# Loading k and q of batches 3 to 7 in slot order, without the ScalarE permutes, and a gate ahead of each k load

## Chip, cores, metric

One core of one Trainium2 chip. The metric is the device time of one execution in microseconds (us), the median over several runs. The engines are PE (TensorE), ACT (ScalarE), DVE (VectorE), POOL (GpSimd) and SP (SyncE); in the views PEld is PE's loading of weights, and SPq is SP's issuing of a DMA. All times of whole kernels here are of fast runs; there were no slow ones (the kernel `isolated` ran once and has no state).

## The reference

```python
# q, k, v: (8 batches, 8 heads, 576 rows, 64), float32
kv  = np.einsum('bhsd,bhse->bhde', k, v)
out = np.einsum('bhsd,bhde->bhse', q, kv)
out = out / np.sqrt(np.mean(out * out, axis=-1, keepdims=True) + 1e-06) * g_norm
x = out.transpose(0, 2, 1, 3).reshape(8, 576, 512)
xn = (x - mu) / np.sqrt(var + 1e-06) * g_ln                       # mean and variance of each row of x
result = x + np.maximum(xn @ w_ch1, 0.0) @ w_ch2                  # 512 -> 2048 -> 512
```

The two large products of the last line are most of PE's work. The attention ahead of them is small, but each 128-row tile needs its q transposed, which is where the changed loads come in.

## The kernel before

A batch's 512 rows lie on 128 partitions, four rows ("slots" t = 0 to 3) to a partition; the last 64 rows come in a load of their own. k and q are loaded by head (1024 rows of 256 elements, cast from float32 to bf16 on the way), and ACT then permutes them from (head, slot) to (slot, head) order, so that one slot of two heads is one 128x128 matmul operand:

```python
def load_kv(buf, src, b, h0=0, h1=H):      # 128 partitions x 8 heads = 1024 rows of 4 x 64 elements
    ...
        nc.gpsimd.dma_start(
            kv_view(buf, b)[:, h0:h1, :, :].rearrange("p h t d -> p h (t d)"),
            src[b, h0:h1, 0:n, :].rearrange("h (p t) d -> p h (t d)", t=t))

def k_permute(eng, b, h0, h1):             # half of the heads: 128x1024 on ACT; q_permute is alike
    ...
    copy(eng, kp[b % 2][0:src.shape[0], 0:t, h0:h1, :],
         src[:, h0:h1, :, :].rearrange("p h t d -> p t h d"))

def q_turn_dma(b):                         # "the turn": a DMA transpose, issued by SP
    att[b]["qT"] = work.tile([128, 20, 128], bf16, tag="qT", name="qT", bufs=3)
    nc.sync.dma_start_transpose(
        att[b]["qT"], qp[b % 2].rearrange("p t h d -> p (t h d)"))
```

The order of the instructions on each engine isn't the order of the source. Every operation is a step with estimated durations, and a small list scheduler lays the steps out in time before the program is emitted:

```python
def run_plan():
    ...
    def ready(s):
        r = 0.0
        ...
        for d in s.deps:
            if d.done is None:
                return None
            r = max(r, d.done + (s.lag if d.dma else 0.0))   # lag: extra time granted to a load
        ...
    ...                                     # for each engine: the earliest ready step, ties by key
```

So the place of a permute among ACT's other instructions follows from when the plan expects its load to have landed. The chip then runs that order whatever the load really does. Batch b's part of the plan, cut:

```python
            gate(f - 7 if b > 3 else 5)      # POOL copies one element of a tile's xT: a wait
            gate_turn()                      # b == 3 only: POOL waits for the turn of batch 2
            pool_load(("k", b), load_kv(kb, k, b), rate4, dk)
            ...
            def some_q():
                gate(f - 6 if b > 3 else 6)
                pool_load(("q", b), load_q(b, 0, 4), rate4, [adone[b - 1]["qread"]])
                ...
            def some_v():
                gate(f - 5 if b > 3 else 7)
                pool_load(("v", b), load_kv(vb, v, b), rate4, dk)
                ...
            for h0, h1 in ((0, 4), (4, 8)):
                kperm.append(add("ACT", 0.85, 1.0, ok - 16, load["k", b][0:1] + dk,
                                 lambda h0=h0, h1=h1: k_permute(nc.scalar, b, h0, h1)))
            ...                              # two q permutes in the same way
            for x in kperm + qperm:
                x.lag = 4.0 if b == 2 else 6.0
            ...
            turn = add_dma("SP", ok - 12, qperm + load["q", b] + (...),
                           lambda: q_turn_dma(b), 2.6e3, 1.0, occ=2.98, lat=0.25, tail=0.42)
```

A second DMA transpose, "the x turn" (xT<-xc), turns the normalized rows for the first-layer matmuls. It stands in SP's order too.

Of the kernel before, what the change touches and what calls it, by code (L numbers as in the profile page):

```python
# [14 lines left out]
def kernel(  # L15
# [11 lines left out]
    nc = tc.nc  # L27
# [6 lines left out]
    B, H, S, D = q.shape  # L34
# [27 lines left out]
    def no_fifth(b):  # L62
        return fifth(b + 1)
# [30 lines left out]
    def add(eng, occ, dur, key, deps, fn, dma=None, alloc=None, main=False, lag=0.0):  # L94
        s = Step()
        s.eng, s.occ, s.dur, s.key, s.fn = eng, occ, dur, key, fn
        s.deps = [d for d in deps if d is not None]
        s.dma, s.alloc, s.main, s.frees, s.behind = dma, alloc, main, None, None
        s.start = s.done = None
        s.lag = lag  # L100
        steps.append(s)
        return s
# [76 lines left out]
    def act_cost(n):  # L179
        return n / 1400 + 0.115, n / 1400 + 0.23  # L180
# [4 lines left out]
    def add_dma(eng, key, deps, fn, nbytes, rate, occ=None, lat=None, tail=None):  # L185
        if eng == "POOL":
            s = add(eng, occ or 0.67, 0, key, deps, fn, dma=(1.0, nbytes / rate / 1e3, 0.6))
        else:
            s = add(eng, occ or 0.55, 0, key, deps, fn,
                    dma=(0.6 if lat is None else lat, nbytes / rate / 1e3,  # L190
                         0.75 if tail is None else tail))
        return s
# [21 lines left out]
    kb = [consts.tile([128, H * 6 * D], bf16, name=f"kb{i}") for i in range(2)]  # L214
# [3 lines left out]
    kp = [consts.tile([128, 6, H, D], bf16, name=f"kp{i}") for i in range(2)]  # L218
    qp = [consts.tile([128, 5, H, D], bf16, name=f"qp{i}") for i in range(2)]
    mark = consts.tile([128, 1], bf16, name="mark")  # L220
    kv_pack = [consts.tile([128, HP, 128], bf16, name=f"kv_pack{i}") for i in range(3)]

    def kv_view(buf, b):
        if b < 2:
            return buf[b % 2][0:96, :].rearrange("p (h t d) -> p h t d", h=H, t=6)
        return buf[b % 2][:, 0:H * 4 * D].rearrange("p (h t d) -> p h t d", h=H, t=4)

    def load_kv(buf, src, b, h0=0, h1=H):
        t = 6 if b < 2 else 4
        n = 576 if b < 2 else 512  # L230
        def fn():
# [3 lines that stand above are left out]
        return fn, n * (h1 - h0) * 256  # L235

    def load_q(b, t0, t1):
        def fn():
            nc.gpsimd.dma_start(
                qb[:, :, t0:t1, :].rearrange("p h t d -> p h (t d)"),  # L240
                q[b, :, 0:512, :].rearrange("h (p t) d -> p h t d", t=4)[:, :, t0:t1, :]
                .rearrange("p h t d -> p h (t d)"))
        return fn, 128 * H * (t1 - t0) * 256
# [7 lines left out]
    def load_slot(dst, src, b, t, h0=0, h1=H):  # L251
        def fn():
            nc.gpsimd.dma_start(
                dst[:, t, h0:h1, :],
                src[b, h0:h1, 0:512, :].rearrange("h (p t) d -> p t h d", t=4)[:, t, :, :])
        return fn, 128 * (h1 - h0) * 256


    groups = []
# [24 lines left out]
    att = [dict() for _ in range(B)]  # L284
    done = [dict() for _ in range(N_TILES)]
    adone = [dict() for _ in range(B)]


    rate6, rate4, rate1 = 400.0, 395.0, 305.0
# [24 lines left out]
    def pool_load(name, fnb, rate=425.0, deps=()):  # L314
        fn, nb = fnb
        s = add_dma("POOL", 0, deps, fn, nb, rate)
        load.setdefault(name, []).append(s)
# [59 lines left out]
    def k_permute(eng, b, h0, h1):  # L377
        src = kv_view(kb, b)
        t = src.shape[2]
        copy(eng, kp[b % 2][0:src.shape[0], 0:t, h0:h1, :],  # L380
             src[:, h0:h1, :, :].rearrange("p h t d -> p t h d"))
# [275 lines left out]
    def plan_batch(b):  # L657
        p = pos[FIRST[b]]
        ok = okey[FIRST[b]]
        kperm = []  # L660
        if b == 1:
            for h0, h1 in ((0, 4), (4, 8)):
                kperm.append(add("ACT", 1.2, 1.35, p - 18, load["k", 1],
                                 lambda h0=h0, h1=h1: k_permute(nc.scalar, 1, h0, h1)))
            for t in range(5):
                key = (p - 17 + 3 * t) if t < 4 else pos[8] - 40
                if t < 4:
                    qperm = add("ACT", *act_cost(512), key, load["q", 1],
                                lambda t=t: q_permute(nc.scalar, 1, t, t + 1))
                    qread = qperm  # L670
                else:
                    qperm = load["q", 1, 4][0]
                add_q_turn_pe(1, t, [qperm, z1[1]], key + 1, ("DVE", "ACT")[t % 2])
            vdeps = load["v", 1]
            adone[1]["qread"] = qread
            adone[1]["qfree"] = adone[1]["qT", 4][0]
        else:
            f = FIRST[b]
            def gate(n):

                if b >= 3:
                    m, i = divmod(n, 4)
                    pool_do(0.1, lambda: nc.gpsimd.tensor_copy(  # L683
                        mark, blk[m]["xT"][:, 0, i * 128:i * 128 + 1]), done[n]["xT"])
            def gate_turn():
                if b == 3:
                    pool_do(0.1, lambda: nc.gpsimd.tensor_copy(
                        mark, att[2]["qT"][:, 0, 0:1]), [adone[2]["qfree"]])
            dk = [adone[b - 2]["kvmm"]]
            if b < 4:  # L690

                pool_do(0.5, lambda: nc.gpsimd.memset(kp[b % 2][no_fifth(b), 4, :, :], 0.0), dk)
            gate(f - 7 if b > 3 else 5)
            gate_turn()
            pool_load(("k", b), load_kv(kb, k, b), rate4, dk)
            pool_load(("k", b), load_fifth(kp[b % 2][:, 4, :, :], k, b), 180.0, dk)
            def some_q():
                gate(f - 6 if b > 3 else 6)
                pool_load(("q", b), load_q(b, 0, 4), rate4, [adone[b - 1]["qread"]])
                pool_load(("q", b), load_fifth(qp[b % 2][:, 4, :, :], q, b), 180.0,  # L700
                          [adone[b - 2]["qfree"]])
            def some_v():
                gate(f - 5 if b > 3 else 7)
                pool_load(("v", b), load_kv(vb, v, b), rate4, dk)
                pool_load(("v", b), load_fifth(v5[b % 2], v, b), 100.0, dk)
            for load_some in (some_v, some_q) if b == 2 else (some_q, some_v):
                load_some()
            for h0, h1 in ((0, 4), (4, 8)):
                kperm.append(add("ACT", 0.85, 1.0, ok - 16, load["k", b][0:1] + dk,
                                 lambda h0=h0, h1=h1: k_permute(nc.scalar, b, h0, h1)))  # L710
            qperm = []
            for t0, t1 in ((0, 2), (2, 4)):
                qperm.append(add("ACT", 0.85, 1.0, ok - 14, load["q", b][0:1] + [
                    adone[b - 2]["qfree"]], lambda t0=t0, t1=t1: q_permute(nc.scalar, b, t0, t1)))
            for x in kperm + qperm:
                x.lag = 4.0 if b == 2 else 6.0
            kperm += load["k", b]
            turn = add_dma("SP", ok - 12, qperm + load["q", b] + (
                adone[b - 3].get("outs", []) if b >= 3 else []),
                           lambda: q_turn_dma(b), 2.6e3, 1.0, occ=2.98, lat=0.25, tail=0.42)  # L720
            for t in range(5):
                adone[b]["qT", t] = [turn]
            adone[b]["qfree"] = turn
            adone[b]["qread"] = qperm[-1]
            vdeps = load["v", b]
        outs_before = adone[b - 3].get("outs", []) if b >= 3 else []
        s = add("PE", 1.12 if b > 1 else 1.34, 1.35 if b > 1 else 1.57, (p - 17.5 if b == 1 else ok - 4), vdeps + kperm,
                lambda: kv_mm(b, range(HP)), alloc="kvt")
        a = add("DVE", 0.34, 0.38, (p - 17 if b == 1 else ok - 2), [s, z1[4], z1[5]] + outs_before,
                lambda: kv_out(b, 0, HP, nc.vector, False))  # L730
        a2 = add("DVE", 0.34, 0.38, (p - 17 if b == 1 else ok - 2), [a], lambda: kv_out(b, 0, HP, nc.vector, True))
        s.frees = a2
        s.lag = 5.0 if b > 2 else 2.0 if b == 2 else 0.0
        adone[b]["kvmm"] = s
        adone[b]["kv"] = [a2]
# [203 lines left out]
```

## Time and profile before

| | before |
|---|---|
| time, median of 3 runs | 298.25 us (298.1 to 299.0) |
| span of the profiled run | 297.3 us |
| PE busy / ACT busy / POOL busy | 282.9 / 159.3 / 54.9 us |
| PE waits listed after 53 us | 1.8 us (ACT) and 0.9 us (turn of batch 3) |

PE's idle time and its waits, with their lines, are read in the prediction. Two cautions for that reading. The profiled run took 299.07 us, more than any of the three timed ones, so its waits may be on the long side. And this trace holds 2017 of PE's 2045 matmul records, and a missing record looks like idle time. I therefore also use a measure that needs no matmul record, the time from the first attention product after 53 us to the start of the last DVE eviction (an eviction takes a matmul's result out of PSUM). Before, it is 239.48 us (53.74 to 293.22). I call it **the stretch**.

### The profile page before, as it was taken

How to read it: one execution, taken by the hardware profiler on the slowest of the kernel's cores; microseconds unless marked ns; L12 is line 12 of the kernel's file. 1: busy time of each engine (PE TensorE's matmuls, PEld its weight loads, DVE VectorE, ACT ScalarE, POOL GpSimd, SP SyncE). 2: the span in 40 equal slices, each digit the busy share in tenths (PEclk: the TensorE clock that was granted, in tenths of full speed). 3: DMA queues.
4: the chain of work that ended last, by engine and by line, in shares of the span. 5: the costliest groups of instructions: out<-in, count | busy, mean ns of one | idle time of the engine just before them, and what ended most of it. 6: DMA issues, size and time to landing. Idle time of an engine off the chain costs nothing.

```text
span 297.3 us, 5131 instructions
## 1 busy us (share of the span) xinstructions
PE 282.9 (95%) x2017; PEld 162.3 (55%) x2045; DVE 165.9 (56%) x359; ACT 159.3 (54%) x308; POOL 54.9 (18%) x88
## 2 busy tenths in 40 slices
PE   3999999999998999799999999999999999999994
PEld 1889955977754445344454444544454444444443
DVE  1497048669695778176754875577557755420022
ACT  3178963978977942594169517841762177016400
POOL 8873320206020122310212020220000000000000
PEclk9999999999999999999999999999999999999999
DMA  7999999549979999994788959888201310120012
GB/s 97 181 200 205 204 198 196 153 90 134 174 134 127 115 113 191 163 155 93 143 129 99 168 143 132 99 92 218 55 18 53 90 53 19 55 90 16 0 73 71
DMA packets 75932, 35.21 MB, mean 118 GB/s; under 512 B 44547, under 2 KB 71427, under 8 KB 75908
## 3 DMA queue, kind: packets, MB, share of 16 engines
q0 software_dynamic: 41888, 18.35, 51.5%
q1 hardware_dynamic: 33860, 16.39, 23.6%
q8 instruction: 16, 0.26, 0.4%
q10 hardware_dynamic: 160, 0.13, 0.2%
q14 instruction: 8, 0.07, 0.1%
HBM read 36.70 MB, written 9.44 MB: 155 GB/s over the span
## 4 chain that ended last, share of the span: by engine, by line
PE 82%; DMA 10%; ACT 2%; issue 1%; DVE 1%; POOL 1%; POOLq 0%
PE mm_ps L609 36%; PE mm_ps L590 28%; PE mm_ps L575 9%; DMA kb<-in_k_dram 3%; PE out_ps L444 3%; DMA qT<-qp 3%; PE kv_ps L421 2%; DMA qp<-in_q_dram 2%; DMA xT<-xc 2%; PE idle_ps L892 1%; ACT m L597 1%; PE qT_ps L393 1%; PE xT_ps L525 1%; POOL kb L232 0%; ACT sq L457 0%
## 5 line engine op out<-in xcount | busy, mean ns | idle before, releaser
L609 PE MATMUL mm_ps<-w,m 128*128 128x512 bf16 (+1 forms) x577 | 129.3, 373 | 0.7
L590 PE MATMUL mm_ps<-xT,w 128*128 128x512 bf16 x435 | 99.8, 379 | 2.4 <-ACT m L597 1.8
L609 PEld LDWEIGHTS <-m 128*128 128x128 bf16 x592 | 56.7, 98 | 59.8
L597 ACT ACTIVATE m<-mm_ps 128x512 bf16<-128x512 f32 x112 | 65.6, 597 | 43.0 <-PE mm_ps L590 42.1
L590 PEld LDWEIGHTS <-w 128*128 128x128 bf16 x448 | 43.1, 98 | 50.6 <-issue 2.1
L466 DVE TENSOR_REDUCE ss<-sq 128x8 f32<-128x512 f32 (+1 forms) x37 | 24.8, 669 | 49.8 <-ACT sq L457 49.8
L616 DVE SCALAR_TENSOR_TENSOR x<-mm_ps,rstd,x 128x512 f32<-128x512 f32 (+1 forms) x37 | 27.1, 734 | 40.0 <-PE mm_ps L609 39.9
L457 ACT ACTIVATE sq<-out_ps 128x512 f32<-128x512 f32 (+1 forms) x37 | 21.5, 585 | 49.4 <-PE out_ps L444 49.4
L575 PE MATMUL mm_ps<-xT,w 128*128 128x128 bf16 x512 | 30.9, 219 | 0.7 <-ACT xT L532 0.7
L575 PEld LDWEIGHTS <-w 128*128 128x128 bf16 x512 | 29.3, 98 | 1.5 <-issue 0.8
L518 DVE SCALAR_TENSOR_TENSOR xc<-x,mv,gl 128x512 bf16<-128x512 f32 (+1 forms) x37 | 27.1, 737 | 1.2
L461 DVE TENSOR_TENSOR xg<-out_ps,gn 128x512 f32<-128x512 f32 (+1 forms) x37 | 24.7, 669 | 0.3
L683 POOL COPY mark<-xT 128x1 bf16<-128x1 bf16 x15 | 5.0, 331 | 100.7 <-DMA xT<-xc 85.3
L582 ACT ACTIVATE m<-mm_ps 128x512 bf16<-128x512 f32 x32 | 18.3, 597 | 2.6 <-PE mm_ps L575 1.9
L496 DVE TENSOR_TENSOR x<-xg,inv 128x512 f32<-128x512 f32 x24 | 16.6, 692 | 0.8
L373 ACT COPY kp<-kb 128x1024 bf16<-128x1024 bf16 (+1 forms) x14 | 15.2, 1102 | 3.2 <-DMA kb<-in_k_dram 3.2
L512 DVE BATCH_NORM_STATS2 stats<-x 128x6 f32<-128x512 f32 x24 | 16.6, 690 | 0.5
L444 PE MATMUL out_ps<-kv_pack,qT 128*128 128x128 bf16 x160 | 15.1, 221 | 1.1 <-DMA qT<-qp 0.9
L444 PEld LDWEIGHTS <-qT 128*128 128x128 bf16 x160 | 11.6, 99 | 8.1 <-DMA qT<-qp 1.4
L470 ACT ACTIVATE rms<-ss,eps_attn 128x8 f32<-128x8 f32 (+1 forms) x37 | 11.1, 300 | 8.7 <-DVE ss L466 8.7
L436 DVE CAST kv_pack<-kv_ps 64x256 bf16<-64x256 f32 (+1 forms) x18 | 7.1, 392 | 13.4 <-PE kv_ps L421 13.1
L421 PE MATMUL kv_ps<-vb,kp 128*128 128x128 bf16 (+1 forms) x144 | 11.7, 234 | 2.6 <-DMA vb<-in_v_dram 2.6
(59 smaller groups left out, 172.6 us busy)
## 6 DMA issues: line engine op xcount, KB each, us to landing
out_dram<-x SPq DMA_DIRECT2D x32, 256.0 KB, 3.0
w<-in_moe_w_ch_dram POOLq DMA_DIRECT2D x8, 512.0 KB, 12.2
qb<-in_q_dram POOLq DMA_DIRECT2D x7, 512.0 KB, 7.4
kb<-in_k_dram POOLq DMA_DIRECT2D x6, 512.0 KB, 8.8
vb<-in_v_dram POOLq DMA_DIRECT2D x6, 512.0 KB, 7.2
out_dram<-x SPq DMA_DIRECT2D x6, 128.0 KB, 2.4
qp<-in_q_dram POOLq DMA_DIRECT2D x10, 64.0 KB, 6.7
kb<-in_k_dram POOLq DMA_DIRECT2D x2, 288.0 KB, 5.8
```

The costliest lines, as they stand in the source:

```text
L421: nc.tensor.matmul(ps[:, hp, :], lhsT=kp[b % 2][p, t, 2 * hp:2 * hp + 2, :].rearrange("p h d -> p (h d)"), rhs=(v5[b % 2][:, 2 * hp:2 * hp ...
L444: nc.tensor.matmul(o3[:, hp, :], lhsT=att[b]["qT"][:, 4 * t + hp, :], rhs=kv_pack[b % 3][:, hp, :], start=(i == 0), stop=(i == len(bs) - 1))
L457: nc.scalar.activation(sq[:, h0:h1, :], st[n]["ps", h0][:, h0:h1, :], func=AF.Square)
L461: nc.vector.tensor_mul(xg[:, h0:h1, :], st[n]["ps", h0][:, h0:h1, :], gn.to_broadcast([128, h1 - h0, D]))
L466: nc.vector.tensor_reduce(ss[:, h0:h1, :], st[n]["sq"][:, h0:h1, :], axis=AX.X, op=ALU.add)
L518: nc.vector.scalar_tensor_tensor(xc[:, f0:f1], in0=st[n]["x"][:, f0:f1], scalar=blk[m]["mv"][:, i, 0:1], in1=gl[:, f0:f1], op0=ALU.subtrac ...
L575: nc.tensor.matmul(ps[:, d, :], lhsT=w1[c][:, kk, d * 128:(d + 1) * 128], rhs=blk[m]["xT"][:, kk, i * 128:(i + 1) * 128], start=(kk == 0), ...
L582: nc.scalar.activation(st[n]["m1"][:, c, :, :], st[n]["m1ps", c], func=AF.Relu)
L590: nc.tensor.matmul(ps, lhsT=w1[c][:, kk, d * 128:(d + 1) * 128], rhs=blk[m]["xT"][:, kk, :], start=(kk == 0), stop=(kk == nKm - 1))
L597: nc.scalar.activation(blk[m]["m1", c][:, d, :], blk[m]["m1ps", g], func=AF.Relu)
L609: nc.tensor.matmul(st[n]["m2ps", f0], lhsT=m1_piece(n, c, d), rhs=w2[c][:, d, f0:f1], start=(c == 0 and d == 0), stop=(c == 3 and d == 3))
L616: nc.vector.scalar_tensor_tensor(x[:, f0:f1], in0=st[n]["m2ps", f0], scalar=blk[m]["rstd"][:, i, :], in1=x[:, f0:f1], op0=ALU.mult, op1=AL ...
```

## The change

Its intent: take 20 permutes off ACT by letting the DMA write k and q in slot order, and keep each k load from running beside the turn of the batch in front. Its diff, with the repeated parts cut:

```diff
+    def load_slots(dst, src, b):
+        def fn():
+            nc.gpsimd.dma_start(
+                dst[:, 0:4, :, :],
+                src[b, :, 0:512, :].rearrange("h (p t) d -> p t h d", t=4))
+        return fn, 128 * H * 4 * 256
...
             def gate_turn():
-                if b == 3:
+                if b >= 3:
                     pool_do(0.1, lambda: nc.gpsimd.tensor_copy(
-                        mark, att[2]["qT"][:, 0, 0:1]), [adone[2]["qfree"]])
+                        mark, att[b - 1]["qT"][:, 0, 0:1]), [adone[b - 1]["qfree"]])
...
-            pool_load(("k", b), load_kv(kb, k, b), rate4, dk)
+            by_slot = b >= 3
+            if by_slot:
+                pool_load(("k", b), load_slots(kp[b % 2], k, b), rate1, dk)
+            else:
+                pool_load(("k", b), load_kv(kb, k, b), rate4, dk)
...
-                pool_load(("q", b), load_q(b, 0, 4), rate4, [adone[b - 1]["qread"]])
+                if by_slot:
+                    pool_load(("q", b), load_slots(qp[b % 2], q, b), rate1, [adone[b - 2]["qfree"]])
+                else:
+                    pool_load(("q", b), load_q(b, 0, 4), rate4, [adone[b - 1]["qread"]])
...
-            for h0, h1 in ((0, 4), (4, 8)):
+            for h0, h1 in ((0, 4), (4, 8))[by_slot * 2:]:
...
-            for t0, t1 in ((0, 2), (2, 4)):
+            for t0, t1 in ((0, 2), (2, 4))[by_slot * 2:]:
...
+            turn.lag = 5.0 if by_slot else 0.0
-            adone[b]["qread"] = qperm[-1]
+            adone[b]["qread"] = qperm[-1] if qperm else None
```

`[by_slot * 2:]` leaves an empty tuple, so that no permute is made. With `turn.lag` the plan lets the turn follow its loads with 5 us to spare; until now it was the permutes that it granted this (`x.lag`).

The diff moves line numbers by 7: L373 becomes L380, L413 L420 (the turn), L421 L428 (k-v product), L444 L451 (attention product), L536 L543 (x turn), L590 L597 (first-layer matmul), and so on. L597 is thus the Relu eviction on ACT in the kernel before, and the first-layer matmul in the kernel after.

## The prediction

> **What bounds the kernel now.** I read the page's busy table first, then PE's waits by stage, then the timeline around each wait.
>
> ```profile
> PE 282.9 (95%) x2017; PEld 162.3 (55%) x2045; DVE 165.9 (56%) x359; ACT 159.3 (54%) x308; POOL 54.9 (18%) x88
> ```
>
> PE is busy for 95% of the span; ACT, whose work the change removes, for 54%. Less ACT work alone is therefore worth nothing; only what ACT makes PE wait for counts. The page warns that a busy PE need not be at its peak. Here it is close: in the timeline, groups of four 128x512 matmuls follow each other every 0.864 us, 216 ns for 512 columns, and the granted clock was 1.00 in all slices. The next view is the table by stage. It covers batches 3 to 7, and then the tail.
>
> ```profile
> core 0: us, PE busy (x) PEld busy (x) DVE busy (x) ACT busy (x) POOL busy (x), PEclk, DMA share, GB/s
> 53.00:297.00 244.00, 236.19 (x1488) 125.09 (x1509) 137.43 (x277) 128.15 (x243) 29.08 (x48) 1.00 0.63 104
> 255.00:297.00 42.00, 37.97 (x189) 18.67 (x191) 6.22 (x9) 9.55 (x16) 0.00 (x0) 0.99 0.16 54
> ```
>
> From 53 us on PE is idle for 244.00 - 236.19 = 7.81 us. Of these 42.00 - 37.97 = 4.03 us lie in the last window, nearly all of it the last eviction and store after the last matmul, which the change doesn't touch. What is left is 7.81 - 4.03 = **3.8 us: the most that any change of these loads can win**. PE's list of waits says where:
>
> ```profile
> PE mm_ps L590 <- ACT m L597: 1.8, 1, 1.8
> ...
> PE out_ps L444 <- DMA qT<-qp: 0.9, 1, 0.9
> ```
>
> One wait of 1.8 us for the Relu eviction, one of 0.9 us for the turned q of batch 3. The other three waits of that list end before 53 us. The first in the timeline:
>
> ```profile
> 123.21 1.04 ACT L373 COPY kp<-kb 128x1024 bf16<-128x1024 bf16 x1 [3.23 <-DMA kb<-in_k_dram]
> 124.16 1.56 ACT L597 ACTIVATE m<-mm_ps 128x512 bf16<-128x512 f32 x3
> 124.81 5.56 PE L590 MATMUL mm_ps<-xT,w 128*128 128x512 bf16 x24 [1.78 <-ACT m L597]
> ```
>
> A k permute of batch 5 stands in ACT's order ahead of evictions that are ready. Its k load was issued at 112.94 and landed 10.25 us later, so ACT stood still for 3.23 us, no PSUM bank of the first layer came free, and PE ran dry for 1.78 us. The load itself was in no hurry: batch 5's k is first multiplied at 148.8. The second:
>
> ```profile
> 81.41 1.98 ACT L373 COPY qp<-qb 128x1024 bf16<-128x1024 bf16 x2
> ...
> 83.64 3.20 SPq L413 DMA_TRANSPOSE qT<-qp  x1
> ...
> 85.39 0.88 POOL L232 DMA_DIRECT2D kb<-in_k_dram  x1
> ...
> 91.68 0.40 PE L444 MATMUL out_ps<-kv_pack,qT 128*128 128x128 bf16 x4 [0.90 <-DMA qT<-qp]
> ```
>
> The turn of batch 3 was issued at 83.64, after the permutes and an output store, and landed 8.00 us later, the slowest of the six (minimum 5.0, median 6.5). The k load of batch 4 was issued 1.75 us after it and ran on the same engines.
>
> **What the Trainium skill says.** (1) "PSUM — Partial Sum Buffer", section "Engine vs sequencer instructions": "ScalarE/VectorE/GpSimdE queues are strict FIFO." The trace agrees: the 3.23 us stand of ACT with evictions behind it. (2) "ScalarE: Activation LUTs", "What ACT_TABLE_LOAD costs": 186 ns plus 0.833 ns an element, so 1039 ns for 1024 elements; the trace has 1042 ns for the permutes. (3) "DMA: Bandwidth & Descriptors", "Specifications" and "Bandwidth": line rate wants transfers of at least 512 B, and the floor of a small load is put at about 10.5 ns a packet. I take that as the price of one more short packet on an engine; no row of this trace isolates it. (4) The same page, "Issuing engines are not separate DMA queues": loads and turns share the 16 engines. The 8.00 us turn beside a load fits.
>
> **The change part by part.**
> Removed on ACT: 4 permutes for each of 5 batches, 20 x 1.042 = **20.8 us of ACT**, of which only the 1.78 us wait (batch 5) and the hold on the batch 3 turn touch PE. ACT should go from 159.3 to about 138.5.
> Added in the loads: ten of them are now cut by head and slot, 128 x 32 = 4096 rows of 64 elements instead of 128 x 8 = 1024 rows of 256. Software-queue packets should grow by 10 x 3072 = 30,720, from 41,888 to 72,608, with the same bytes. An engine gets 256 packets instead of 64, each 256 B read and 128 B written. By the skill's 10.5 ns the 192 further packets are about 2.0 us a load (estimate, upper side, as part of a packet's time is spent on bytes anyway).
> Added on POOL: issuing 512 rows took 688 ns and 1024 rows 882 ns, 0.38 ns a row. By that slope 4096 rows need 882 + 3072 x 0.379 = 2.05 us (estimate), 1.17 us more for each of ten, and four further marks of 0.2 to 0.7 us: POOL goes from 54.9 to about 68, far from a bound.
> Moved: k loads of batches 4 to 7 wait for the turn in front. Only batch 4's is really held, from 85.4 to about 89; batch 5's from 112.9 to about 115. Their k is needed at 117 and 149. On PE the order changes in one place: the k-v product of batch 3 comes two groups (1.73 us) later, still two groups ahead of its first use, so its 0.85 us of kv_pack casts should just fit. On SP the turn of batch 5 moves ahead of one x turn.
>
> Is a q load now late for its turn? Issue of q to issue of the turn was 15.3, 12.3, 14.5, 11.1 and 9.6 us for batches 3 to 7. The new load needs 7.4 (median landing before) + 1.2 (issue) + 2.0 (packets) = 10.6 us. Only batch 7 misses, by 1.0 us, and before 195.85 its turn waited for the permutes anyway. The x turn behind it went out at 201.51; landings in that stage took at most 4.9 us, so it was there by 206.4, and the next block starts at 207.58: 1.2 us to spare. That just holds it.
>
> Sum: 1.78 + 0.90 = 2.7 us won on PE, nothing lost. 298.25 - 2.7 = **295.6 us**, 0.9% faster.
>
> **The rivals.**
> A: *the short rows become the new wait.* If slot loads land in 15 us instead of 10.6, the turn of batch 7 comes 5.4 us late, the x turn behind it in SP's order too, and PE waits some 4 us; batch 6, with 4.5 us to spare at its block, loses little. That gives 295.6 + 4 = about 300. For it: the page's DMA share already stands at 8 or 9 tenths in several slices. Against: bytes are the same, the k loads have 30 us of room, and no k load now competes with the turn in front.
> B: *ACT was a brake everywhere*, so that all 20.8 us matter and the time falls by more than 2%. Against: 3.8 us is all the idle time that PE has outside start and tail; to win 6 us is impossible unless the matmuls themselves become faster.
> C: *the wait moves.* The 1.78 us stall goes, but batch 3's first product then waits for the later k-v product or the casts behind other DVE work (about 0.5 us), or the 0.9 us wait remains since the output store still stands ahead of the turn on SP. That gives 296.5 to 297.5.
>
> **Range and chances.** The ceiling gives 298.25 - 3.8 = 294.5 as the best; timing noise before was 298.1 to 299.0. C sets most of the upper side, A the tail. Range 294.2 to 297.8. Within 2% means 292.3 to 304.2: faster needs the impossible B, 0.02; slower needs an A larger than I can build, 0.03; same 0.95.
>
> **What would show it.** Right: no permutes of 128x1024 after 53 us except batch 2's four, ACT near 138.5; no wait of PE on L597's counterpart near 124 and none at batch 3's first product; about 72,600 packets on the software queue; slot loads of about 2 us issue on POOL and about 10 us to landing; the k load of batch 4 after the turn landed, and that turn nearer 6 us than 8. PE's busy time unchanged at 283, its idle time from 53 us to the tail about 1 us. Wrong: a new PE wait for an x turn or qT (rival A), one for kv_pack (C), or shorter matmuls (B).

## The result, and the profile after

| | before | after |
|---|---|---|
| time, median, same chip | 298.18 us (297.62 to 299.0, 4 runs) | 295.95 us (295.5 to 296.31, 4 runs) |
| ratio of fast runs | | 0.9922 (95%: 0.9894 to 0.9951) |
| profiled span | 297.3 us | 294.5 us |
| the stretch | 239.48 us | 237.39 us |
| ACT / POOL busy | 159.3 / 54.9 us | 143.1 / 66.1 us |

A ratio is the mean time of one kernel's fast runs over that of the other's in the same rounds, so not quite the ratio of the medians. The change is 0.8% faster, which counts as the same at 2%. Of the 2.8 us between the two spans, 2.09 us lie in the stretch. Most of the rest (0.68 us) comes before 53 us, where the change touches nothing: the first attention product after 53 us starts at 53.06 instead of 53.74. I don't count that.

The busy line of the page after:

```profile
PE 283.4 (96%) x2045; PEld 161.2 (55%) x2045; DVE 165.7 (56%) x359; ACT 143.1 (49%) x288; POOL 66.1 (22%) x92
```

PE's work is the same, and ACT has 20 instructions fewer. The software queue, before and after (packets, MB, share of the engines' span):

```profile
q0 software_dynamic: 41888, 18.35, 51.5%
```

```profile
q0 software_dynamic: 72608, 18.35, 64.8%
```

30,720 more packets for the same bytes, the number worked out in advance. PE's waits after (line, what for, us in total, times, longest):

```profile
PE kv_ps L428 <- DMA vb<-in_v_dram: 3.0, 1, 3.0
PE scale_ps L307 <- DMA scales<-in_moe_g_ln_dram: 2.2, 1, 2.2
PE mm_ps L597 <- DMA xT<-xc: 0.8, 1, 0.8
```

These are the three longest. The first two lie in the start-up and stood there before. The waits of 1.8 and 0.9 us are both gone; the third line is new. First the one that went, in the timeline around the turn of batch 3 after (start, us, instruction, and in brackets the idle time before it with its releaser):

```profile
82.33 3.23 SPq L420 DMA_TRANSPOSE qT<-qp  x1
...
88.08 0.19 POOL L694 COPY mark<-qT 128x1 bf16<-128x1 bf16 x1 [4.18 <-DMA qT<-qp]
88.76 2.02 POOL L260 DMA_DIRECT2D kp<-in_k_dram  x1 [0.49 <-PE kv_ps L428]
...
89.95 0.39 PE L451 MATMUL out_ps<-kv_pack,qT 128*128 128x128 bf16 x4
```

The turn is issued 1.31 us earlier than before (83.64), as no permute stands ahead of it (0.68 us of this is the earlier start of everything), and lands after 5.6 us instead of 8.0. The mark on POOL is the added gate: it waits 4.18 us for the turn, so the k load of batch 4 goes out at 88.76 instead of 85.39. PE's first product of the batch at 89.95 has no wait.

Then the new wait, in batch 6. Before:

```profile
162.58 0.88 POOL L232 DMA_DIRECT2D vb<-in_v_dram  x1 [0.27 <-issue]
...
166.18 3.62 SPq L413 DMA_TRANSPOSE qT<-qp  x1
169.89 1.22 SPq L536 DMA_TRANSPOSE xT<-xc  x1
```

After:

```profile
163.52 0.89 POOL L232 DMA_DIRECT2D vb<-in_v_dram  x1 [0.42 <-issue]
163.65 3.38 SPq L420 DMA_TRANSPOSE qT<-qp  x1
167.12 2.19 SPq L543 DMA_TRANSPOSE xT<-xc  x1
...
174.80 4.48 PE L597 MATMUL mm_ps<-xT,w 128*128 128x512 bf16 x20 [0.76 <-DMA xT<-xc]
```

On the clock the turn goes out 2.5 us earlier, and the v load 0.9 us later. But PE is 3.7 us ahead by now (its attention product of 167.61 stands at 163.93): measured by PE's work the turn goes out 1.2 us later, and the v load 4.6 us. They used to be 3.6 us apart; now they start together. The turn lands after 10.4 us (5.1 before), and the x turn behind it after 7.43 us (2.5 before), 0.76 us too late for PE. The chain of work that ended last runs through it:

```profile
167.12 7.43 DMA xT<-xc
174.55 0.25 issue
174.80 4.48 PE mm_ps L597 x20
```

### The profile page after: what moved, and what is told of

It reads as the page before. It is cut to its first block, busy times and chain, and to the rows that moved or that the text cites. A ratio compares the mean times of both kernels' runs of the same rounds, so it can differ in the third digit from the quotient of the medians.

```text
span 294.5 us, 5143 instructions
## 1 busy us (share of the span) xinstructions
PE 283.4 (96%) x2045; PEld 161.2 (55%) x2045; DVE 165.7 (56%) x359; ACT 143.1 (49%) x288; POOL 66.1 (22%) x92
## 3 DMA queue, kind: packets, MB, share of 16 engines
q0 software_dynamic: 72608, 18.35, 64.8%
## 4 chain that ended last, share of the span: by engine, by line
PE 87%; DMA 7%; POOL 3%; DVE 1%; issue 1%; ACT 0%; ACTq 0%; POOLq 0%
PE mm_ps L616 39%; PE mm_ps L597 33%; PE mm_ps L582 8%; DMA w<-in_moe_w_ch_dram 5%; PE kv_ps L428 3%; PE out_ps L451 3%; DMA xT<-xc 3%; POOL qp L253 1%; POOL w L333 1%; PE xT_ps L532 1%; POOL kb L232 1%; POOL vb L232 0%; PE qT_ps L400 0%; DVE ss L473 0%; DVE x L503 0%
## 5 line engine op out<-in xcount | busy, mean ns | idle before, releaser
L597 PE MATMUL mm_ps<-xT,w 128*128 128x512 bf16 x448 | 100.8, 379 | 0.8 <-DMA xT<-xc 0.8
L604 ACT ACTIVATE m<-mm_ps 128x512 bf16<-128x512 f32 x112 | 66.8, 597 | 51.3 <-PE mm_ps L597 50.3
L597 PEld LDWEIGHTS <-w 128*128 128x128 bf16 x448 | 43.0, 98 | 49.6 <-issue 1.2
L589 ACT ACTIVATE m<-mm_ps 128x512 bf16<-128x512 f32 x32 | 18.3, 597 | 3.0 <-PE mm_ps L582 2.3
L451 PEld LDWEIGHTS <-qT 128*128 128x128 bf16 x160 | 11.5, 98 | 7.2 <-DVE kv_pack L443 0.3
L451 PE MATMUL out_ps<-kv_pack,qT 128*128 128x128 bf16 x160 | 15.0, 220 | 0.1
L428 PE MATMUL kv_ps<-vb,kp 128*128 128x128 bf16 (+1 forms) x144 | 11.8, 234 | 3.0 <-DMA vb<-in_v_dram 3.0
L428 PEld LDWEIGHTS <-kp 128*128 128x128 bf16 (+1 forms) x168 | 11.1, 105 | 4.3 <-DVE kp L382 2.3
```

The source lines that it names most:

```text
L428: nc.tensor.matmul(ps[:, hp, :], lhsT=kp[b % 2][p, t, 2 * hp:2 * hp + 2, :].rearrange("p h d -> p (h d)"), rhs=(v5[b % 2][:, 2 * hp:2 * hp ...
L451: nc.tensor.matmul(o3[:, hp, :], lhsT=att[b]["qT"][:, 4 * t + hp, :], rhs=kv_pack[b % 3][:, hp, :], start=(i == 0), stop=(i == len(bs) - 1))
L589: nc.scalar.activation(st[n]["m1"][:, c, :, :], st[n]["m1ps", c], func=AF.Relu)
L597: nc.tensor.matmul(ps, lhsT=w1[c][:, kk, d * 128:(d + 1) * 128], rhs=blk[m]["xT"][:, kk, :], start=(kk == 0), stop=(kk == nKm - 1))
L604: nc.scalar.activation(blk[m]["m1", c][:, d, :], blk[m]["m1ps", g], func=AF.Relu)
```

## The experiments

There are twelve experiments in three calls of one chip each: nine new kernels, and three kernels run again. All but `isolated` were compared with the kernel before in the same rounds; a call had 11 runs of before and 6 of each kernel with five rounds. **Compare kernels inside one call.** On the second chip the kernel before was slower and wider than on the others (299.75 us, 297.3 to 301.44), so that all ratios of that call look better.

| call | kernel | median us (range) | ratio to before (95%) | the stretch | PE wait after 53 us |
|---|---|---|---|---|---|
| 1 | before | 298.21 (297.18 to 300.15) | | | |
| 1 | k_only | 295.77 (295.6 to 296.26) | 0.9914 (0.9885 to 0.9944) | 236.47 | none |
| 1 | q_only | 295.92 (295.58 to 296.36) | 0.9917 (0.9887 to 0.9946) | 236.48 | none |
| 1 | gate_only | 295.51 (295.23 to 295.9) | 0.9905 (0.9873 to 0.9936) | 236.48 | none |
| 1 | no_gate | 296.28 (295.34 to 296.6) | 0.9925 (0.9895 to 0.9955) | 237.03 | 0.4 |
| 2 | before | 299.75 (297.3 to 301.44) | | | |
| 2 | late_b5 | 297.26 (296.8 to 297.85) | 0.9923 (0.988 to 0.9965) | 238.25 | 1.6 |
| 2 | early_b5 | 296.87 (295.72 to 297.39) | 0.9905 (0.986 to 0.9949) | 236.75 | none listed |
| 2 | dummy_act | 296.27 (295.96 to 296.63) | 0.9889 (0.9843 to 0.9935) | 237.27 | 0.5 |
| 2 | v_behind_q | 295.94 (295.61 to 296.5) | 0.9882 (0.984 to 0.9924) | 236.47 | none |
| 3 | before | 298.1 (296.94 to 299.98) | | | |
| 3 | after_again | 296.06 (295.66 to 296.94) | 0.9922 (0.9889 to 0.9955) | 236.89 | 0.3 |
| 3 | v_behind_q_again | 295.7 (295.42 to 295.83) | 0.9905 (0.9873 to 0.9936) | 236.48 | none |
| 3 | gate_only_again | 295.76 (295.38 to 296.05) | 0.9904 (0.9869 to 0.9938) | 236.47 | none |

The stretch is one profiled run each. That six profiles with no wait (four kernels, two of them on two chips) agree on 236.47 or 236.48 makes it a good ruler: it is the floor that PE's own work sets there, and what stands above it is lost to waits.

The theory: the gain is the two waits, not ACT's work. The first experiments do one part alone, or leave one out.

**k_only**: k by slot, q as before, gate for batch 3 only.

```diff
-            by_slot = b >= 3
+            k_slot = b >= 3      # used where k is loaded and permuted
+            q_slot = b >= 99     # used where q is loaded and permuted
-                if b >= 3:       # in gate_turn
+                if b == 3:
```

> Only the k loads of batches 3 to 7 go by slot; q keeps its permutes, no new gate. Theory (only PE's two waits count: 1.8 us for the k permute of batch 5 that stands in ACT, 0.9 us for the turn of batch 3): the 1.8 us wait goes, the 0.9 us wait stays, since the q permutes and the k load beside the turn stay; 298.2 - 1.8 = 296.4 us, ratio 0.994. Rival (ACT work as such is the brake, so the gain goes by permutes removed): half of the whole gain, 1.1 us, 297.1 us. Also: ACT busy falls by 10 x 1.04 us.

Measured: 295.77 us where 296.4 was expected, no PE wait. The first half of the expectation held; the remaining wait at batch 3 did not come. Its turn was issued at 82.97 and landed after 5.3 us, although the k load of batch 4, now a slot load, was issued at 85.07, two microseconds behind it. A slot load so close behind a turn did not slow it, which is followed up below.

**q_only**: the same with k_slot at 99 and q_slot at 3.

> Only the q loads of batches 3 to 7 go by slot; k keeps its permutes, no new gate. Theory: the k permute of batch 5 still stands in ACT's order, so PE's 1.8 us wait stays; the turn of batch 3 still meets the k load of batch 4, so at most half of the 0.9 us is won: 297.5 to 298.2 us, ratio 0.998 to 1.000. Rival (ACT work as such): the same as for k alone, 297.1 us.

Measured: 295.92 us. **A miss.** All ten k permutes are still there, but no stand of ACT at batch 5: the permute now starts at 123.81 with its data long there. The plan had put it later among the evictions, because other steps had moved.

**gate_only**: the kernel before, with all 20 permutes, plus the gate alone (both at 99, gate at b >= 3).

> The kernel before with the new gate alone: k loads of batches 4 to 7 wait for the turn in front; all permutes stay. Theory: the turn of batch 3 lands in under 7 us instead of 8.0 and the 0.9 us wait goes; but the k load of batch 5 starts some 2 us later (115 instead of 112.9), so its permute stands longer in ACT and PE's 1.8 us wait grows to about 4: net 298.2 - 0.9 + 2.2 = 299.5 us, ratio 1.004. Rival (gates cost nothing, loads have room): 297.3 us.

Measured: 295.51 us, the fastest of the call. **A clear miss**, for the same reason, and the most instructive. Holding back the k load of batch 5 should have made ACT stand even longer, had its order been fixed. Its timelines on POOL and ACT:

```profile
112.33 0.89 POOL L232 DMA_DIRECT2D kb<-in_k_dram  x1 [0.72 <-issue]
```

```profile
123.75 0.60 ACT L604 ACTIVATE m<-mm_ps 128x512 bf16<-128x512 f32 x1 [0.27 <-PE mm_ps L597]
124.25 1.04 ACT L380 COPY kp<-kb 128x1024 bf16<-128x1024 bf16 x1
125.18 1.76 ACT L604 ACTIVATE m<-mm_ps 128x512 bf16<-128x512 f32 x3
```

The load landed 8.6 us after its issue, at 120.9; the permute stands behind nine first-layer evictions of its block (two in the kernel before) and starts at 124.25 with no wait. The plan knows of the gate, so it expected the load later and put the permute later. It was the **order**, not the load, that the gate changed here: in its old place, behind the eviction that ends at 118.1, the permute would still have stood 2.8 us for this load (3.23 before). At batch 3 the gate did what it was meant for: the k load went out at 88.42, and the turn issued at 82.80 landed after 5.0 us.

**no_gate**: the whole change with the gate of before.

```diff
-                if b >= 3:
+                if b == 3:
```

> The changed kernel without the new gate (k loads of batches 4 to 7 as early as before); order on the other engines is the same. Theory: the 1.8 us stay won; the k load of batch 4 runs beside the turn of batch 3 again, which takes about 8 us and lands near 90.3, 0.4 us after it is needed: 296.3 us, 0.3 to 0.5 us slower than the change, ratio to before 0.9935. Rival (the gate is what pays): the 0.9 us comes back whole or more, 296.9 us or above.

Measured: 296.28 us. The turn of batch 3 took 5.6 us, not 8, with the slot load of batch 4 issued at 84.96 (turn at 82.56). **The number was hit by luck**: the wait at batch 3 that I had reckoned with did not come, and the 0.4 us in the table is the wait of batch 6, at 174.66. The change has the ratio 0.9922 in both its comparisons and this kernel 0.9925, on other chips: with slot loads no worth of the gate can be told; with head loads it is not tested alone, as gate_only moved the order too.

All three parts alone remove the stand of batch 5. To show that the order is the cause, the next two kernels move nothing but batch 5's k permutes in the plan.

**late_b5**: the kernel before, with the two k permutes of batch 5 planned later.

```diff
             for x in kperm + qperm:
                 x.lag = 4.0 if b == 2 else 6.0
+            if b == 5:
+                for x in kperm:
+                    x.lag = 12.0
```

> The kernel before with nothing but the two k permutes of batch 5 planned later: in ACT's order the first stands behind nine first-layer evictions of its block instead of behind two (one kv_pack neighbour and one x turn swap places too; PE and POOL are in the same order). Loads, permutes and gates as before. Theory (the wait came from where that one permute stands in ACT's order, not from ACT work or from the form of the load): the 1.8 us wait goes, the 0.9 us wait for the turn of batch 3 stays: 298.2 - 1.8 = 296.4 us, ratio 0.994. Rival (it takes less ACT work, or another load, to win it): 298.2 us, ratio 1.000.

Measured: 297.26 us. The 1.8 us wait is gone with every permute and every load in its old form; the other wait stays, and is even longer in this profile, as the turn took 8.7 us. PE's list and the permute:

```profile
PE out_ps L444 <- DMA qT<-qp: 1.6, 1, 1.6
```

```profile
126.41 1.04 ACT L373 COPY kp<-kb 128x1024 bf16<-128x1024 bf16 x1
```

The stretch is 238.25 us, 1.78 above the floor, nearly the one wait left. Apart from ACT's, the built orders differ from before's in two places, one DVE instruction and one x turn; PE's and POOL's are the same. So in the times position alone is enough for the first term: the mean is 2.4 us below before's in the same rounds, and 1.7 us below that of before's seven runs whose clock was not at 0.994. This profile alone wouldn't show it. In it the k load of batch 5 landed at 119.9 (issued at 111.92, 8.0 us), before ACT would have reached the permute in its old place. How long ACT stands there hangs on two things, the place of the permute and the landing of its load, and the landing differs from profile to profile. (gate_only is the profile in which the old place would have cost a stand.)

**early_b5**: gate_only with that permute put back behind two evictions; the orders of all other engines are those of gate_only.

```diff
+            if b == 5:
+                for x in kperm:
+                    x.lag = 0.0
```

> The gate-only kernel (295.5 us) with the first k permute of batch 5 put back to where the kernel before has it, behind two first-layer evictions; order on all other engines as in gate-only. Theory: its load lands near 120.9, so ACT stands from 118.1 to 120.9 and PE loses about 1.4 us again: 296.9 us. Rival (gate-only is fast because of the gate itself, wherever the permute stands): 295.5 us.

Measured: 296.87 us, near the 296.9 that was expected (on the chip where before was slower). ACT's stand is back:

```profile
118.10 0.60 ACT L604 ACTIVATE m<-mm_ps 128x512 bf16<-128x512 f32 x1 [1.38 <-PE mm_ps L597]
120.27 1.04 ACT L380 COPY kp<-kb 128x1024 bf16<-128x1024 bf16 x1 [1.56 <-DMA kb<-in_k_dram]
```

But the profiled run was one of the quicker ones (296.12 us): the load landed at 120.3, ACT stood 1.56 us, no wait of PE is listed, and the stretch is 0.28 us above the floor. In the kernel before PE lost 1.78 us of a stand of 3.23, so some 1.45 us of a stand cost PE nothing (estimate), and the two profiles roughly agree. The six runs spread from 295.72 to 297.39, wider than any other variant, and their mean is 0.7 us above that of v_behind_q in the same rounds. That the time now hangs on when that load lands fits this, but how long ACT stood in the slower runs, and whether PE waited, isn't shown.

**dummy_act**: the change plus 20 copies of 128x1024 on ACT that nobody needs and that wait for nothing.

```diff
+    junkp = consts.tile([128, 1024], bf16, name="junkp")
...
+            if by_slot:
+                for h0 in (0, 4):
+                    add("ACT", 0.85, 1.0, ok - 16, load["k", b][0:1] + dk, lambda h0=h0: copy(
+                        nc.scalar, junkp.rearrange("p (t h d) -> p t h d", t=4, h=4),
+                        kv_view(kb[0:1] * 2, 2)[:, h0:h0 + 4, :, :].rearrange("p h t d -> p t h d"))).lag = 6.0
+                ...                        # and two of qb in the same way
```

> The changed kernel with 20 copies of 128x1024 on ACT put back where the permutes of batches 3 to 7 would stand, from buffers that are long full to a spare tile, so that they wait for no load: ACT's work of before, without its waits. Theory: ACT busy back to about 163 us, time unchanged within 0.3 us: 295.9 us, ratio 0.992. Rival (ACT work as such): back towards 298 us.

Measured: 296.27 us; the change itself has 295.95 and 296.06 in other calls, and v_behind_q, below, is 0.2 us faster by its mean in this one. The page and the groups of its copies:

```profile
PE 282.2 (96%) x2017; PEld 161.0 (55%) x2045; DVE 166.1 (56%) x359; ACT 160.8 (55%) x308; POOL 65.5 (22%) x92
```

```profile
L381 ACT COPY junkp<-qb 128x1024 bf16<-128x1024 bf16 x10 | 10.5, 1048 | 0.1
L381 ACT COPY junkp<-kb 128x1024 bf16<-128x1024 bf16 x10 | 10.4, 1038 | 0.1
```

ACT is as busy as before the change and the gain is still there. Its one PE wait (0.5 us) is for the x turn, as in the change. ACT's work as such costs nothing that these runs can tell.

**v_behind_q**: the change, with the v load of batches 3 to 7 moved up behind the q load, out of the turn's way.

```diff
             def some_v():
-                gate(f - 5 if b > 3 else 7)
+                if not by_slot:
+                    gate(f - 5 if b > 3 else 7)
                 pool_load(("v", b), load_kv(vb, v, b), rate4, dk)
```

> The changed kernel with the gate of the v loads of batches 3 to 7 taken out: each v load goes right behind its q load; all else in the same order. Theory for the new 0.8 us wait (the v load of batch 6 was issued in the same 0.2 us as the turn of batch 6, which took 10.4 us, and the x turn behind it landed late): no v load meets the turn any more, the turn lands in under 7 us and the wait goes: 295.2 us. Rival (the short rows of q themselves make turn or x turn late): 295.9 us or more.

Measured: 295.94 us. By the number alone that is the rival's (295.9 or more; 295.2 was the theory's), on the chip where before was slower too; call 3 has 295.7. The trace decides. On POOL and SP:

```profile
157.12 1.23 POOL L232 DMA_DIRECT2D vb<-in_v_dram  x1
```

```profile
165.36 3.76 SPq L420 DMA_TRANSPOSE qT<-qp  x1
169.21 1.22 SPq L543 DMA_TRANSPOSE xT<-xc  x1
```

The v load is issued 8 us ahead of the turn of batch 6, which lands after 5.7 us instead of 10.4. PE has no wait after 53 us, and the stretch is at the floor, with q still loaded by slot; the repeat shows the same (5.8 us). The built orders differ from the change's in the five marks on POOL alone. That settles the cause of the new wait: the v load beside the turn. Being beside it makes the turn slow, not always PE: in q_only the v load also came 0.9 us behind the turn of batch 6 (161.39), which took 9.9 us, and PE did not wait, as the turn had gone out 2.3 us earlier than in the change.

**isolated**: a kernel of its own, wrong on purpose, in which the loads and the turn run alone and then together, with a mark on POOL that waits for both between the phases.

```python
for phase in ("a", "s", "a", "s", "t", "t", "ta", "ts", "ta", "ts"):
    for what in phase:           # a: k load of 1024 rows, s: slot load of 4096 rows, t: turn
        ...
    both()                       # POOL reads one element of kp and one of qT
```

> No attention at all (the result is wrong on purpose): one load or turn at a time, each phase waiting for the one before it: a load of 1024 rows, one of 4096 rows, both again, two turns alone, then a turn issued together with a 1024-row load, with a 4096-row load, and both again. My estimate of the short rows: 0.88 and 2.05 us of issue, landing 1.2 + 2.0 = 3.2 us later than the 1024-row load alone. Rival (rows cost only their issue): 1.2 us later. Turn: 5.0 us alone; beside a load of either form 8 us or more if sharing the engines is what made it slow; beside the 4096-row load nearer 5 if only the start of that load is later.

Measured, first the loads alone, in POOL's timeline:

```profile
23.84 0.88 POOL L48 DMA_DIRECT2D kp<-in_k_dram  x1 [0.18 <-POOL mark L61]
29.70 0.19 POOL L60 COPY mark<-kp 128x1 bf16<-128x1 bf16 x1 [4.99 <-DMA kp<-in_k_dram]
...
30.19 2.00 POOL L53 DMA_DIRECT2D kp<-in_k_dram  x1 [0.18 <-POOL mark L61]
37.64 0.19 POOL L60 COPY mark<-kp 128x1 bf16<-128x1 bf16 x1 [5.45 <-DMA kp<-in_k_dram]
```

The load of 1024 rows lands 5.8 us after its issue began (the other one: 6.0), that of 4096 rows after 7.4 (7.6). Of the 1.6 us between them 1.12 are the longer issue (2.00 instead of 0.88); the 3072 further rows themselves cost about 0.5 us. Then the turn: alone, beside a load of 1024 rows, and beside one of 4096 rows, each with its time to landing.

```profile
L57 SPq DMA_TRANSPOSE qT<-qp x1: 3006/3006/3006, 38.0 to 38.0; - x1
...
DMA to landing us min/median/max: 4.9/4.9/4.9
```

```profile
L57 SPq DMA_TRANSPOSE qT<-qp x1: 3040/3040/3040, 48.4 to 48.4; - x1
...
DMA to landing us min/median/max: 8.3/8.3/8.3
```

```profile
L57 SPq DMA_TRANSPOSE qT<-qp x1: 3008/3008/3008, 57.6 to 57.6; - x1
...
DMA to landing us min/median/max: 6.7/6.7/6.7
```

Their second instances took 4.9, 8.2 and 6.4 us. A plain load beside a turn costs the turn 3.3 to 3.4 us, a slot load 1.5 to 1.8, though it has four times the rows. Its issue takes 1.1 us longer, so its packets begin later; that this is why it disturbs less is likely, not shown. My estimate for the rows (3.2 us later) missed, and the rival (1.2) was nearer; the 8 us or more that I expected beside either form came with the plain load only. Why the turn of batch 6 in the change lost more than that, about 5.5 us (10.4 against 4.9), stays open.

**after_again, v_behind_q_again, gate_only_again**: the change and the two best variants on one chip, for the difference between them.

> The changed kernel itself, on the same chip as the next two. From the first product after 53 us to the last eviction its trace should again lie about 0.9 us above the 236.47 us that four variants without any PE wait reached, with the wait for the x turn near 174.8; 0.3 us slower than the other two.

> As before: no wait of PE after 53 us, 236.47 us from the first product after 53 us to the last eviction, 0.3 to 0.8 us faster than the changed kernel on this chip.

> The kernel before with the gate alone: 236.48 us from the first product after 53 us to the last eviction, within 0.3 us of the run with v behind q, and 0.3 to 0.8 us faster than the changed kernel, although it keeps all 20 permutes on ACT.

Measured: means of 296.19, 295.69 and 295.71 us. Both variants beat the change by 0.5 us (0.17%) and before by 2.7. The two can't be told apart: gate_only, a version that still has all 20 permutes, is as fast as one that has none. The change's six runs alone spread over 1.28 us, so this difference rests on few runs. In this profile of the change the turn of batch 6 took 10.3 us again, and PE waited at the same matmul:

```profile
174.30 4.48 PE L597 MATMUL mm_ps<-xT,w 128*128 128x512 bf16 x19 [0.26 <-DVE x L503]
```

The view puts it down to an x of DVE. But the x turn issued at 166.20 landed 7.9 us later, at 174.1, and PE went on 0.2 us after that, as it did in the first profile (174.55 and 174.80). I take it for the same wait, 0.26 us this time; no_gate's 0.4 us is alike (landed at 174.4, PE at 174.66). The stretch is above the floor each time (237.39, 236.89), but less than expected here (0.4 us, not 0.9).

## Why the prediction was right

295.6 us was predicted, with the range 294.2 to 297.8; 295.95 was measured (296.06 in the repeat). By its own steps:

- **The ceiling and what bounds the kernel**: right, but 3.8 us was too much. By their means no variant won more than 2.9 us on the first and third chip, and 3.6 (299.61 to 296.03) on the second, where the kernel before ran worse. Over the stretch PE was idle for 4.03 us before, in a trace with 2017 records; v_behind_q_again, also with 2017 and without a wait, shows 1.36 us there, and gate_only, with 2045, shows 0.04. So about 1.3 us of the idle time were missing records, and 2.7 us (4.03 - 1.32) to 3.0 (239.48 - 236.48) could be won. Two smaller readings were off without harm: four other waits of PE end before 53 us, not three, and the clock was 0.99 in the last window.
- **The 1.78 us wait of batch 5**: right in cause, incomplete in what removes it. The strict order of ACT behind one early permute is shown by late_b5 (moved: faster, no wait) and, for ACT alone, by early_b5 (moved back: ACT stands again). Its size is that of one profile, in which the load took 10.25 us; in other profiles with this load it took from 7.3 (early_b5) to 10.1 us (q_only). But I credited the removal of the permutes. Any change that shifted the plan did it too.
- **The 0.90 us wait of batch 3**: right. Before, the turn ran beside a k load of 1024 rows (8.0 us, and 8.3 or 8.2 isolated against 4.9 alone). An earlier turn, the gate and the slot form act together, and in k_only, q_only and no_gate some of them suffice.
- **ACT to 138.5 us**: it fell by 16.2 us to 143.1, not by 20.8. I multiplied 20 by the length of one. Busy time counts overlaps once, and neighbours on ACT overlap: in gate_only's lines the eviction ends at 124.35 while the permute starts at 124.25, and the next eviction starts at 125.18 while the permute ends at 125.29. Some 0.2 us a permute, 4 us for 20 (estimate), fit the gap. In dummy_act 20 such copies added 17.7 us.
- **POOL to about 68 us, packets to 72,608, issue of 2.05 us**: 66.1, 72,608 and 2.01 to 2.02 (2.3 to 2.4 for the three of ten that were issued right behind another load).
- **10.6 us to landing of a slot load**: a little too long. The medians in the kernel were 9.9 us (q, for which it was worked out) and 8.2 (k). The term of 2.0 us for the packets was mis-sized; the isolated loads show about 0.5.
- **"nothing lost"**: wrong, the one step on the way to the time that failed. Of rival A the second half came, a late turn and a late x turn behind it, at batch 6, where I had counted 4.5 us to spare, not at batch 7. Its first half did not: the cause was not the short rows but that the turn and a v load came to run side by side. I had checked when each load would be late for its turn, and not what each turn would now run beside. It cost 0.3 to 0.8 us in the profiles and 0.5 us in the times. 2.7 won less 0.5 lost gives 2.2, and 298.18 - 295.95 is 2.23. So close a match is partly luck: the ratio's interval allows 1.5 to 3.2 us, and the 2.7 was read in a run of 299.07 us and taken off a median of 298.25.
- **Rival B** (ACT as a brake everywhere) is refuted by dummy_act. **Rival C** did not come: no profile shows PE waiting for kv_pack after 53 us. (after_again lists 0.3 us of it, at 12.78 us in the start-up, as gate_only does.)

What stays open: in the records, six of the 33 runs of before in the three calls had a mean granted clock of 0.994 and took 299.45 to 301.44 us; no variant's run was below 0.996. Whether PE's wait of 1.8 us or something else sets this off no profiled run shows. It can be a part of the mean difference, and of why before is the noisier kernel.

## What to carry to other kernels

When one engine is busy for 95% of the span, add up its waits first: that sum bounds what any change elsewhere can give, and taking work off another engine is worth only the waits that this work causes. In an in-order queue the place of an instruction matters more than its length: one permute a few evictions too early cost 1.8 us in the profiled run, twenty well placed ones nothing that could be told; so before giving an instruction to the DMA, try moving it, and where a plan sets the order, compare the built orders of each variant before reasoning about it (two of my expectations, q_only and gate_only, failed on that). After any change that shifts transfers, look at what each transfer now runs beside, above all DMA transposes on which the bound engine waits.

## What the Trainium skill lacked or had wrong

- "DMA: Bandwidth & Descriptors", section "Issuing engines are not separate DMA queues": it says that transfers interleave on the same 16 engines, which the runs agree with, but has no size for it. A DMA transpose of 128x2560 bf16 took 4.9 us alone, 8.3 and 8.2 beside a load of 1024 rows, and 6.7 and 6.4 beside one of 4096 rows.
- The same page, section "Anatomy of one DMA — SWDGE (gpsimd) path": descriptor generation, called small and variable, has no size for each row. The issue on POOL, which I take for it, is the larger part of what short rows cost a load here: it took 0.88 us for 1024 rows and 2.00 for 4096, about 0.36 ns a row.
- The same page, section "Bandwidth": the 10.5 ns a packet, a floor of a small load, doesn't serve as the price of each further packet of a long one: it gave 2.0 us for 192 more packets an engine, and the isolated loads showed about 0.5.
